# Attention and a bilinear feed-forward on one core: the first eight units' products with v made in pairs, and the early feed-forward columns split around the turning

## The chip, the core and the metric

The kernel runs on one core of one Trainium2 chip. The metric is the device time of one execution in microseconds (us); the kernel before took 1402.33 us (median of three runs, 1402.2 to 1406.92). Five engines work side by side, each through its own list of instructions in order, and wait for one another on semaphores: PE (TensorE, the matrix multiplier), ACT (ScalarE), DVE (VectorE), POOL (GpSimd) and SP, which here only issues DMAs. PE writes to PSUM alone; ACT and DVE fetch its results from there. A difference of 0.5% (about 7 us) is taken as what a measurement of this kernel can tell from no change.

## The reference

For 8 batches of 8 heads, with 576 rows of 64 columns, softmax attention in which a score counts only if it is within tau of its row's maximum; then, with the heads laid side by side (x has 4608 rows and 512 columns), a bilinear feed-forward.

```python
scores = scale * np.matmul(q, k.transpose(0, 1, 3, 2))
thresh = np.max(scores, axis=-1, keepdims=True) - tau
scores = np.where(scores >= thresh, scores, -1000000000.0)
scores = scores - np.max(scores, axis=-1, keepdims=True)
attn = np.exp(scores)
attn = attn / (np.sum(attn, axis=-1, keepdims=True) + 1e-09)
attn_out = np.matmul(attn, v)
...
a = x @ w_a
b = x @ w_b
return (a * b @ w_out)
```

The weights w_a and w_b are 512 by 1536, w_out is 1536 by 512.

## The kernel before

**Units and slots.** Two heads make a pair; there are 32 pairs, four to a batch. A unit is a pair and 128 of its rows (the last 64 rows of two pairs share a unit of their own). The main loop (L1117) goes over units in slots g = 0, 1, 2, ...; the first eight units are pairs 0 to 3 with rows 0 to 127 (g = 0 to 3) and pairs 0 to 3 with rows 128 to 255 (g = 4 to 7). Slot g holds the scores of unit g and later steps of the units before it. Each engine's instructions stand in the order in which the loop issues them (`keep_order`), so the loop fixes the order of every engine's list.

**One slot, for the first units.** In program order:
- `scores` (L389): PE makes the scores of unit g for both heads (L404) in two PSUM tiles; DVE takes the row maxima (L411, one per head) and the threshold (L412).
- for g = 2 to 9, `weighted_unit` (L594) for unit g - 2: `product` (L538) multiplies the turned weights with v in 36 PE matmuls (L546) of 64 moving columns each, a 64 by 64 block of v being the stationary side; ACT fetches the first half of the result (L553, 128x64) and DVE the second in two copies (L554, 64x64), into the feed-forward's input x; POOL copies x with its partition halves exchanged into xS (L569, two copies of 64x128).
- `convert_rest` and `convert_first`: the feed-forward's weights come as 64-bit words of which ACT (L298, L299), POOL (L305, L324) and DVE (L311, L319) make fp32 numbers, two or three pieces a slot in this stretch.
- `weigh` (L422): ACT makes the exponentials (L431, L432), DVE applies the threshold and sums (L435); then DVE's reciprocal.
- `turn_pe` (L472) for unit g - 1 (up to g = 8): PE turns and scales the weights with 18 matmuls against a diagonal matrix (L483) into two PSUM tiles, of which ACT copies the larger (L485) and DVE the smaller (L486). The result is what `weighted_unit` reads in the next slot.
- `diagonals` (L456) on ACT for unit g (L462).
- `advance(pace)` (L1204): feed-forward work on the first block of x, once it is there (from g = 5), by columns: a slot's allowance is 0.04 of a block's columns plus 576, and each product with v takes 576 off. In the first feed-forward steps (L854) PE multiplies the weights with x or xS; ACT fetches the product with w_a (L860), and DVE multiplies in the one with w_b (L862).

From g = 9 on another scheme takes over: the weights are turned by DVE (L502) and DMAs through DRAM, and `advance` stands at four places of a slot.

**PSUM.** All PE results share one pool of four tiles (`banks`, L128), taken in turn. A new tile can be written once the tile taken four before it has been read: so the order in which PE's steps stand decides which copy each step waits for.

**Loads.** SP issues the loads in order: v of a pair (`load_v`, L214) one slot ahead of the pair's first use here, and pieces of weights (`load_weights`, L271) between them, each behind the PE instruction last issued before it.

The functions that the diff touches, and what calls them:

Of the kernel before, what the change touches and what calls it, by code (L numbers as in the profile page):

```python
# [23 lines left out]
BY_PE = 8  # L24
# [30 lines left out]
def kernel(  # L55
# [38 lines left out]
    nc = tc.nc  # L94
    B, H, S, D = q.shape
    P = 128
# [3 lines left out]
    HP = H // 2  # L100
    NT = 4
    MAIN = NT * P
    TAIL = S - MAIN
# [8 lines left out]
    NSLOT = 9  # L112
# [15 lines left out]
    def banks(n, name):  # L128

        return psum.tile([P, 2, 512], FP32, tag="banks", name=name)[:, :, 0:n]  # L130
# [4 lines left out]
    loaded = {}  # L135
# [90 lines left out]
    for f in range(NG):  # L226
        for c in range(HP):
            for dst, w in ((wa_sb, w_a), (wb_sb, w_b)):
                src = []
                for r in range(2):  # L230
                    chunks = [(2 * c + e) % HP * 2 + (r + (c >= HP // 2)) % 2 for e in range(2)]
                    cols = slice(f * CW + r * CH, f * CW + (r + 1) * CH)
                    rows = w[:, cols].bitcast(U32).rearrange("(k p) f -> p k f", p=D)
                    src.append(rows[:, chunks[0]:chunks[1] + 1:2])
                pieces.append((dst[:, f, 2 * c:2 * c + 2].rearrange("p k f -> p (k f)"), src))
    for F in range(NF):
# [3 lines left out]
    state = {"loaded": 0, "added": 0, "converted": 0, "rows": 0, "sums": False, "through": 0, "over": False,  # L240
             "layer": False, "paced": False, "all": False, "turn": 0, "due": NPIECES, "wide": True, "slot": 0, "reading": False, "first": 0}
# [90 lines left out]
    for _ in range(TW_BUFS):  # L332
        t = work.tile([P, 2 * NB, Q], FP32, tag="tw", bufs=TW_BUFS, name="rows")
# [21 lines left out]
    prepared, scored, weights, turned, whole = {}, {}, {}, {}, {}  # L355
    x_of, xtail_of = {}, {}
    ahead, settled, settled_of = {}, {}, {}
    blocks, complete, swaps = [], [], {}
# [113 lines left out]
    def turn_pe(i, u):  # L472

        ws, dg = weights.pop((i, u))
        ws = [w.rearrange("p n e -> p (n e)") for w in ws]
        wT = turned_tile()[:, 0:G].rearrange("p g s e -> p (g s e)").rearrange("p (s w) -> p s w", w=P)
        turned[i, u, "pe"] = [wT[:, :, y * D:(y + 1) * D] for y in range(2)]
        tp = banks(512, "tp").rearrange("p y (s q) -> p y s q", s=NT)
        last = banks(P, "tp")
        for s in range(NSLOT):  # L480
            for j, w in enumerate(ws):
                to = (last[:, 0] if s == 2 * NT else tp[:, s // NT, s % NT])[j * D:(j + 1) * D]
                nc.tensor.matmul(to, w[:, s * D:(s + 1) * D], dg[:, j], start=True, stop=True)  # L483
        for y in range(2):
            nc.scalar.copy(wT[:, y * NT:(y + 1) * NT], tp[:, y])  # L485
        nc.vector.tensor_copy(wT[:, 2 * NT], last[:, 0])  # L486
# [51 lines left out]
    def product(wT, vm, n):  # L538

        pv = banks(n // 2, "pv")  # L540
        for s in range(NSLOT):
            for j in range(2):
                rows = slice(j * D, (j + 1) * D)
                for c in range(2):
                    y = j ^ c
                    nc.tensor.matmul(pv[c * D:(c + 1) * D, y], vm[rows, s], wT[y](rows, s),  # L546
                                     start=(s == 0), stop=(s == NSLOT - 1))
        return pv

    def settle(out, pv, c0, c1, others):  # L550

        n = c1 - c0
        one = [nc.scalar.copy(out[:, 0:n], pv[:, 0, c0:c1])]  # L553
        two = [nc.vector.tensor_copy(out[c * D:(c + 1) * D, n:2 * n], pv[(1 - c) * D:(2 - c) * D, 1, c0:c1])  # L554
               for c in range(2)]
        for mine, theirs in ((one, others[1] + two), (two, others[0] + one)):
            for a in mine:
                for b in theirs:
                    tc.declare_no_dep(a.ins, b.ins, reason="banks of their own")
        others[0].extend(one)  # L560
        others[1].extend(two)

    def x_tile(name):
        return work.tile([P, HP, HALF], FP32, tag="xT", bufs=XT_BUFS, name=name)

    def exchange(x, xs, hp, c0, c1, engine):

        for r in range(2):
            engine.tensor_copy(xs[r * D:(r + 1) * D, hp, c0:c1], x[(1 - r) * D:(2 - r) * D, hp, c0:c1])  # L569
# [21 lines left out]
                    exchange(x_of[key], xs, hp, 0, HALF, nc.gpsimd)  # L591
                ahead[key] = xs, count

    def weighted_unit(i, u):  # L594

        b, hp = pairs[i]
        wT = turned.pop((i, u, "pe"))
        pv = product([lambda rows, s, t=t: t[rows, s] for t in wT], loaded[i]["v"], P)
        settled_of[i] = settled_of.get(i, 0) + P
        if (b, 0) not in x_of:  # L600
            x_of[b, 0] = x_tile("xT")
            state["xs"] = x_tile("xS")
        settle(x_of[b, 0][:, hp, u * P:(u + 1) * P], pv, 0, D, ([], []))
        exchange(x_of[b, 0], state["xs"], hp, u * P, (u + 1) * P, nc.gpsimd)
        if hp == HP - 1:
            state["rows"] = u + 1
            if u == 0:
                blocks.append(((x_of[b, 0], state["xs"]), ("first", b, 0)))

    def tails(x, pv, hp, c0, c1):  # L610

        copies = [(nc.scalar.copy if j == c else nc.vector.tensor_copy)(
            x[j * D:(j + 1) * D, hp + c, c0:c1], pv[c * D:(c + 1) * D, j]) for c in range(2) for j in range(2)]
        for n, a in enumerate(copies):
            for m, b in enumerate(copies[:n]):
                if (n in (0, 3)) != (m in (0, 3)):
                    tc.declare_no_dep(a.ins, b.ins, reason="partitions of their own")

    def weighted_tails(i):

        b, hp = pairs[i]
        flush(("v", i), ("v", i + 1), ("wT", i, 2))
        t = turned.pop((i, NT))
        pv = banks(TAIL, "pv")
        for s in range(NSLOT):
            for j in range(2):
                rows = slice(j * D, (j + 1) * D)
                for c in range(2):
                    nc.tensor.matmul(pv[c * D:(c + 1) * D, j], loaded[i + c]["v"][rows, s],
                                     t[rows, 2 * c:2 * c + 2, s], start=(s == 0), stop=(s == NSLOT - 1))  # L630
        if hp == 0 and b % GT == 0:
            xtail_of[b // GT] = x_tile("xt")
        t = b % GT
        tails(xtail_of[b // GT], pv, hp, t * TAIL, (t + 1) * TAIL)
        for p in (i, i + 1):
            settled_of[p] = settled_of.get(p, 0) + TAIL
            if settled_of[p] == S:
                del loaded[p], prepared[p]
# [385 lines left out]
    def advance(cols):  # L1024
        running["owed"] += cols
        while running["owed"] > 0:
            if running["ffn"] is None:
                exchange_blocks()
                if not blocks:
                    running["owed"] = 0.0  # L1030
                    return
                if len(blocks[0][0]) == 4 and state["first"] == 3 * SEVENS:
                    for group in range(SEVENS):
                        first_sums(3, group)
                    state["first"] += 1
                if state["over"] and not state["all"]:
                    first_sums(3, SEVENS)
                    state["all"] = True
                running["tiles"] = len(blocks[0][0])
                running["ffn"] = ffn(*blocks.pop(0))  # L1040
                running["left"] = cost()
            step, rest, whole = next(running["ffn"], (None, 0, 0))
            if step == 0:
                running["owed"] = 0.0
                return
            if step is None:
                running["ffn"] = None
                state["through"] += 1
            else:
                running["owed"] -= step  # L1050
                running["left"] -= step
                passed(step)
                running["done"] = running["done"] + step if rest else 0
                running["rest"] = rest
                running["room"] = min(ROOM, whole // 2)
# [24 lines left out]
    units = []  # L1080
# [9 lines left out]
    first = {i: g for g, (i, u) in enumerate(units) if u == 0}  # L1090
# [21 lines left out]
    n = 0  # L1112
# [4 lines left out]
    for g in range(len(units) + PV_LAG):  # L1117
# [9 lines left out]
        if BY_PE + 1 < g <= len(units) + 1:  # L1127
            n = g - PV_LAG
# [3 lines left out]
        if here:  # L1132
            i, u = units[g]
# [4 lines left out]
        pace = (PACE if g > BY_PE else PACE_EARLY) * BLOCK_COLS  # L1138
        if g > BY_PE:
            pace = min(pace, backlog() / (min([a for a in arrivals if a > g] + [len(units) + PV_LAG + 1]) - g))  # L1140
        pace += NSLOT * S / (2 * NT + 1) + CATCH_UP * max(backlog() - BLOCK_COLS, 0)
        if 2 <= g < BY_PE + 2:
            weighted_unit(*units[g - 2])
            running["owed"] -= NSLOT * P // 2
        if g < 3:
            prep_copy(*prep_pe(g + 1, "q"))
# [20 lines left out]
        if g < 3:  # L1167
            kT, tp = prep_pe(g + 1, "k")
            nc.scalar.copy(kT.rearrange("p (c k) -> p c k", c=2), tp)
        if 0 < g <= BY_PE:  # L1170
            turn_pe(*units[g - 1])
        if g > BY_PE:
            n = g - PV_LAG
# [27 lines left out]
            normalise(i, u)  # L1201
        convert_rest(g, 1)
        if g <= BY_PE:
            advance(pace)  # L1204
        convert_rest(g, 2)
        for n in early.get(g, [])[1:]:
            convert_first(n)
# [74 lines left out]
```

## Time and profile before

| | us |
|---|---|
| time, median of three runs | 1402.33 |
| time of the profiled execution | 1400.57 |
| its span, first to last instruction | 1398.8 |
| PE busy | 1361.5 (97%) |
| DVE busy | 1013.9 (72%) |
| ACT busy | 680.8 (49%) |
| POOL busy | 492.8 (35%) |

The profiled execution's time is 1.77 us above its span. Busy PE is not PE at its peak, since matmuls are pipelined; a share over the whole span is a mean over stages with different limits. In a timeline line the first number is the start and the second the length in us, xN the number of instructions merged into the line, and the bracket at the end the idle time of the engine just before it with what ended that. PE records a matmul of fp32 numbers twice, so 36 matmuls are 72 records.

### The profile page before, as it was taken

Reading aid. Unit: us, or ns where it says so; the run is one execution under the profiler, and the core shown is the slowest. Engines: PE = TensorE matmul, PEld = TensorE weight load, DVE = VectorE, ACT = ScalarE, POOL = GpSimd, SP = SyncE. Lnnn points to the kernel's source line nnn. Section 1 sums busy time; section 2 is a strip of 40 time slices with the busy share of each in tenths; the row PEclk is TensorE's granted clock in tenths of the full one; section 3 lists DMA queues with packets and bytes.
Section 4 is the critical chain, followed back from the end, with each engine's and each line's share of the span. In section 5 each row is a group of like instructions: output and inputs, shape, how many; then the busy total and the mean of one; then the engine's idle time right before and its main releaser. Section 6 shows DMA issues by size and latency. Waiting matters only on the chain.

```text
span 1398.8 us, 76307 instructions
## 1 busy us (share of the span) xinstructions
PE 1361.5 (97%) x33836; PEld 1258.5 (90%) x33836; DVE 1013.9 (72%) x2205; ACT 680.8 (49%) x1248; POOL 492.8 (35%) x675
## 2 busy tenths in 40 slices
PE   7889999999999999999999999999999999999998
PEld 5677588999998799999999999998899998799998
DVE  6999877787777768786767776778777776745425
ACT  6977555545554555544454545454545455431110
POOL 2764543424150607060515142332515060708100
PEclk9999999999999999999999999999999999999999
DMA  9977876667666775676556775566656775550000
GB/s 211 241 212 223 204 206 173 174 170 187 174 154 168 190 192 155 176 190 160 143 143 160 186 180 159 136 190 169 181 130 161 199 190 154 137 146 19 4 19 18
DMA packets 327449, 223.21 MB, mean 160 GB/s; under 512 B 171600, under 2 KB 311632, under 8 KB 327120
## 3 DMA queue, kind: packets, MB, share of 16 engines
q1 hardware_dynamic: 323936, 216.95, 60.1%
q8 instruction: 266, 4.36, 1.3%
q10 hardware_dynamic: 3184, 1.38, 0.4%
q14 instruction: 63, 0.52, 0.1%
HBM read 128.58 MB, written 89.65 MB: 156 GB/s over the span
## 4 chain that ended last, share of the span: by engine, by line
PE 88%; DMA 5%; DVE 4%; SPq 2%; issue 1%; ACT 1%; ACTq 0%; DVEq 0%
PE pab L750 29%; PE po L920 22%; PE pab L854 18%; PE sc L404 9%; PE pv L546 9%; SPq L144 1%; DMA vm<-in_v_dram 1%; DMA wT<-swap 1%; DVE tw L435 1%; DVE mx L411 1%; DMA more_u<-in_moe_w_a_dram 1%; DVE low L311 0%; DMA more_u<-in_moe_w_b_dram 0%; DVE tw L502 0%; DMA sums_u<-in_k_dram 0%
## 5 line engine op out<-in xcount | busy, mean ns | idle before, releaser
L454 ACT ACTIVATE tw<-tw,rcp 128x576 f32<-128x576 f32 x272 | 196.1, 768 | 201.3 <-DVE rcp L448 201.3
L411 DVE TENSOR_REDUCE mx<-sc 128x1 f32<-128x576 f32 x288 | 204.6, 752 | 121.2 <-PE sc L404 120.9
L432 ACT ACTIVATE tw<-sc,bias,scalars 128x576 f32<-128x576 f32 x288 | 239.6, 832 | 10.4 <-DMA qT<-in_q_dram 0.4
L712 POOL TENSOR_TENSOR h<-h,u 128x512 f32<-128x512 f32 x28 | 35.2, 1277 | 590.4 <-DVE h L824 414.1
L435 DVE SCALAR_TENSOR_TENSOR tw<-sc,thr,tw 128x576 f32<-128x576 f32 x288 | 220.9, 797 | 12.3 <-ACT tw L432 11.9
L920 PE MATMUL po<-wo_sb,h 64*64 64x256 f32 (+1 forms) x3408 | 210.5, 367 | 0.0
L502 DVE STREAM_TRANSPOSE tw<-tw 128x576 f32<-128x576 f32 x272 | 194.4, 752 | 0.8 <-ACT tw L454 0.8
L920 PEld LDWEIGHTS po<-wo_sb,h 64*64 64x64 f32 x3408 | 169.8, 133 | 14.9
L404 PE MATMUL sc<-kT,qT 64*64 64x288 f32 x2016 | 170.3, 404 | 1.8 <-issue 0.9
L546 PE MATMUL pv<-wT,vm 64*64 64x128 f32 (+2 forms) x4896 | 164.0, 275 | 3.7 <-DMA vm<-in_v_dram 1.4
L546 PEld LDWEIGHTS pv<-wT,vm 64*64 64x64 f32 x4896 | 153.2, 133 | 12.0 <-issue 4.0
L920 PE MATMUL po<-sums_u,h 64*64 64x256 f32 x2448 | 156.6, 376 | 0.0
L883 POOL TENSOR_TENSOR h<-h 128x256 f32<-128x256 f32 x168 | 117.2, 731 | 110.9 <-PE po L920 106.1
L750 PE MATMUL pab<-xU,wb_sb 64*64 64x128 f32 x4352 | 137.8, 269 | 0.0
L920 PEld LDWEIGHTS po<-sums_u,h 64*64 64x64 f32 x2448 | 126.1, 133 | 12.3 <-DVE h L862 0.5
L750 PEld LDWEIGHTS pab<-xU,wb_sb 64*64 64x64 f32 x4352 | 133.3, 133 | 1.8 <-ACT h L806 0.5
L404 PEld LDWEIGHTS sc<-kT,qT 64*64 64x64 f32 x2016 | 108.8, 133 | 17.3 <-issue 4.9
L431 ACT ACTIVATE bias<-mx,scalars 128x1 f32<-128x1 f32 x288 | 82.7, 287 | 66.1 <-DVE mx L411 65.6
L553 ACT COPY xT<-pv 128x128 f32<-128x128 f32 (+1 forms) x68 | 17.6, 259 | 193.5 <-PE pv L546 193.5
L750 PE MATMUL pab<-xS,wa_sb 64*64 64x128 f32 x2176 | 108.5, 269 | 0.8 <-issue 0.8
L554 DVE COPY xT<-pv 64x128 f32<-64x128 f32 (+1 forms) x136 | 38.1, 280 | 80.5 <-PE pv L546 79.0
L535 ACT COPY kept<-po 128x512 f32<-128x512 f32 x65 | 34.8, 535 | 120.3 <-PE po L920 106.4
(163 smaller groups left out, 2468.7 us busy)
## 6 DMA issues: line engine op xcount, KB each, us to landing
wT<-swap SPq DMA_DIRECT2D x242, 288.0 KB, 3.8
swap<-tw SPq DMA_DIRECT2D x480, 144.0 KB, 3.1
vm<-in_v_dram SPq DMA_DIRECT2D x128, 72.0 KB, 2.6
swap<-tw SPq DMA_DIRECT2D x128, 72.0 KB, 2.9
kT<-in_k_dram SPq DMA_DIRECT2D x112, 72.0 KB, 3.2
wT<-swap SPq DMA_DIRECT2D x56, 144.0 KB, 3.6
out_dram<-kept SPq DMA_DIRECT2D x27, 256.0 KB, 3.7
qT<-in_q_dram SPq DMA_DIRECT2D x112, 40.0 KB, 2.8
```

The lines of the kernel that those rows point to most:

```text
L404: nc.tensor.matmul(sc[m][o * D:o * D + wide, c], qT[r, q0:q0 + wide], kT[r, c * SH:(c + 1) * SH], start=True, stop=True)
L411: nc.vector.tensor_reduce(mx[:, c], sc[j], axis=AX.XY, op=ALU.max)
L431: nc.scalar.activation(bias[:, j:j + 1], mx[:, j:j + 1], AF.Copy, scale=e_nscale)
L432: nc.scalar.activation(wb[j], sb[j], AF.Exp, bias=bias[:, j:j + 1], scale=e_scale)
L435: nc.vector.scalar_tensor_tensor(out=wv, in0=sb[j], scalar=thr[:, j:j + 1], in1=wv, op0=ALU.is_ge, op1=ALU.mult, accum_out=sums[:, j:j + 1])
L454: nc.scalar.activation(w, w, AF.Copy, scale=rcp[:, j:j + 1])
L502: nc.vector.transpose(w, w)
L546: nc.tensor.matmul(pv[c * D:(c + 1) * D, y], vm[rows, s], wT[y](rows, s), start=(s == 0), stop=(s == NSLOT - 1))
L750: nc.tensor.matmul(out[c * D:(c + 1) * D, r, f * P:(f + 1) * P], w[g][k][rows, w0:w0 + D], moving[k][rows], start=(fresh and k == 0 and f ...
L854: nc.tensor.matmul(pab[c:c + columns(), r], w[rows, f // n, k, fs + c:fs + c + columns()], moving, start=(k == 0), stop=(k == H - 1))
L883: (nc.vector if state["over"] else nc.gpsimd).tensor_tensor(*a, **kw)
L920: nc.tensor.matmul(po[c * D:(c + 1) * D, r, y, cut], ht[rows, t0:t0 + D], other[rows, f, cut], start=(f == 0), stop=(f == NF // 2 - 1))
```

## The change

**Products in pairs.** Units (i, u) and (i + 1, u) of two neighbouring pairs are now multiplied with v together, in slots 3, 5, 7 and 9, and slots 2, 4, 6 and 8 have no product. `by_pairs` makes 36 matmuls of 128 columns for both units: output partitions 0 to 63 belong to the first pair and 64 to 127 to the second, where before they were two halves of one unit's columns. The result is fetched as `tails` (L610) does it: two copies of 64x128 by ACT and two by DVE for a pair of units. POOL exchanges both pairs at once, in two copies of 64 x 2 x 128. The feed-forward's allowance is still lessened by 576 in every slot from 2 to 9. `weighted_tails` calls `by_pairs` too, with what it did before.

**Feed-forward columns.** Up to slot 8, `advance(pace)` behind the turning becomes `advance(pace / 2)` ahead of `turn_pe` and `advance(pace / 2)` at the old place.

```diff
@@ turn_pe
-        turned[i, u, "pe"] = [wT[:, :, y * D:(y + 1) * D] for y in range(2)]
+        turned[i, u, "pe"] = wT
@@
-    def weighted_unit(i, u):
+    def weighted_units(i, u):
         b, hp = pairs[i]
-        wT = turned.pop((i, u, "pe"))
-        pv = product([lambda rows, s, t=t: t[rows, s] for t in wT], loaded[i]["v"], P)
-        settled_of[i] = settled_of.get(i, 0) + P
+        wT = [turned.pop((i + c, u, "pe")) for c in range(2)]
+        pv = by_pairs(P, i, lambda rows, c, s: wT[c][rows, s])
...
-        settle(x_of[b, 0][:, hp, u * P:(u + 1) * P], pv, 0, D, ([], []))
-        exchange(x_of[b, 0], state["xs"], hp, u * P, (u + 1) * P, nc.gpsimd)
-        if hp == HP - 1:
+        x, xs, cols = x_of[b, 0], state["xs"], slice(u * P, (u + 1) * P)
+        tails(x, pv, hp, cols.start, cols.stop)
+        for r in range(2):
+            nc.gpsimd.tensor_copy(xs[r * D:(r + 1) * D, hp:hp + 2, cols], x[(1 - r) * D:(2 - r) * D, hp:hp + 2, cols])
+        for p in (i, i + 1):
+            settled_of[p] = settled_of.get(p, 0) + P
+        if hp + 1 == HP - 1:
...
+    def by_pairs(n, i, moving):
+        pv = banks(n, "pv")
+        for s in range(NSLOT):
+            for j in range(2):
+                rows = slice(j * D, (j + 1) * D)
+                for c in range(2):
+                    nc.tensor.matmul(pv[c * D:(c + 1) * D, j], loaded[i + c]["v"][rows, s], moving(rows, c, s),
+                                     start=(s == 0), stop=(s == NSLOT - 1))
+        return pv
@@ main loop
         if 2 <= g < BY_PE + 2:
-            weighted_unit(*units[g - 2])
+            if g % 2:
+                weighted_units(*units[g - 3])
             running["owed"] -= NSLOT * P // 2
...
+        if g <= BY_PE:
+            advance(pace / 2)
         if 0 < g <= BY_PE:
             turn_pe(*units[g - 1])
...
         if g <= BY_PE:
-            advance(pace)
+            advance(pace / 2)
```

From slot 10 on, the lists of all engines are the same as before, with the same waits.

More of the change, by code (lines that the diff above doesn't have):

```diff
@@ L602, in weighted_unit @@
             state["xs"] = x_tile("xS")
-        settle(x_of[b, 0][:, hp, u * P:(u + 1) * P], pv, 0, D, ([], []))
-        exchange(x_of[b, 0], state["xs"], hp, u * P, (u + 1) * P, nc.gpsimd)
-        if hp == HP - 1:
+        x, xs, cols = x_of[b, 0], state["xs"], slice(u * P, (u + 1) * P)
[5 more added lines that the diff above has]
+        if hp + 1 == HP - 1:
             state["rows"] = u + 1
             if u == 0:
-                blocks.append(((x_of[b, 0], state["xs"]), ("first", b, 0)))
+                blocks.append(((x, xs), ("first", b, 0)))
+    def by_pairs(n, i, moving):
[7 more added lines that the diff above has]
+        return pv
     def tails(x, pv, hp, c0, c1):
@@ L623, in weighted_tails @@
         t = turned.pop((i, NT))
[L624 to L630, printed above, removed]
+        pv = by_pairs(TAIL, i, lambda rows, c, s: t[rows, 2 * c:2 * c + 2, s])
         if hp == 0 and b % GT == 0:
```

## Prediction

> **What bounds the kernel now.** I read the busy tenths by slices first, for where time is lost.
>
> ```profile
> PE   7889999999999999999999999999999999999998
> ...
> DVE  6999877787777768786767776778777776745425
> ...
> PE 88%; DMA 5%; DVE 4%; SPq 2%; issue 1%; ACT 1%; ACTq 0%; DVEq 0%
> ```
>
> PE is full from the fourth slice of 35 us on, and the chain of waits is PE for 88%. PE idles 37 us in all (1398.8 - 1361.5). Then the busy time by stages of 20 us, to see who holds the beginning (columns: busy us of PE, PEld (weight loads), DVE, ACT, POOL with counts; PE clock; DMA share; GB/s).
>
> ```profile
> 40.00:60.00 20.00, 15.00 (x349) 13.07 (x341) 19.19 (x41) 17.42 (x37) 15.33 (x20) 1.00 1.09 237
> 60.00:80.00 20.00, 16.48 (x339) 14.63 (x337) 19.57 (x45) 17.86 (x37) 15.46 (x18) 0.96 0.84 231
> 80.00:100.00 20.00, 17.94 (x316) 16.05 (x314) 18.42 (x38) 15.00 (x31) 13.51 (x14) 0.96 0.71 205
> 100.00:120.00 20.00, 18.57 (x284) 17.03 (x282) 19.40 (x40) 15.69 (x31) 10.84 (x11) 1.00 0.87 252
> ```
>
> Up to about 140 us DVE is the bound: 19.19 and 19.57 of 20 us busy, where PE has 15.00 and 16.48. Slots 2 to 9, the ones changed, lie between 22 and 91 us. So a change there is worth what it takes from DVE's list or from DVE's few waits; PE time saved there lies beside DVE. From slot 10 on all lists and waits are as before, so whatever is won or lost by slot 9 shifts the rest as a whole: DVE stays busy up to 141 us, and then PE runs a fixed amount of work to the end.
>
> The timeline shows the two waits of DVE that matter, one in slot 3 and one in slot 9.
>
> ```profile
> 32.87 1.26 PE L546 MATMUL pv<-wT,vm 64*64 64x64 f32 x68 [0.56 <-DMA vm<-in_v_dram]
> ...
> 34.18 0.46 DVE L554 COPY xT<-pv 64x64 f32<-64x64 f32 x2 [0.66 <-PE pv L546]
> ```
>
> ```profile
> 78.36 2.08 PE L854 MATMUL pab<-xT,wa_sb 64*128 64x128 f32 x16 [1.45 <-DVE tw L435]
> ...
> 80.20 1.81 PE L854 MATMUL pab<-xS,wa_sb 64*128 64x128 f32 x16
> ...
> 83.89 1.42 DVE L411 TENSOR_REDUCE mx<-sc 128x1 f32<-128x576 f32 x2 [1.43 <-PE sc L404]
> ```
>
> In slot 3 the product waits for v of pair 1, and DVE for the product. In slot 9 DVE waits 1.43 us for scores, because PE before them ran at half clock: these groups of 16 records take 1.16 and 1.06 us elsewhere. The granted clock says so:
>
> ```profile
> 77.00:78.00 1.00, 0.00 (x0) 0.00 (x0) 1.00 (x3) 1.00 (x3) 0.86 (x3) 1.00 0.75 307
> 78.00:79.00 1.00, 0.64 (x6) 0.67 (x8) 1.00 (x5) 0.89 (x3) 1.00 (x2) 0.66 0.01 4
> 79.00:80.00 1.00, 1.00 (x13) 1.00 (x13) 0.93 (x3) 0.77 (x2) 0.57 (x1) 0.50 0.00 0
> ```
>
> The clock (third figure from the end) falls to 0.50 after PE had stood still for 0.96 and 1.45 us with 0.44 us of work between.
>
> **The change part by part.**
>
> *PE.* Eight products of 64 columns take 1.28 us each, 10.2 us; four of 128 columns take 2.20 us each (the row of 72 such records at 113.27 us), 8.8 us. The saving of 1.4 us lies where DVE is the bound: nothing by itself.
>
> *DVE's copies.* Each product of a unit cost two copies of 64x64, 0.46 us, 0.49 with the gap behind. A pair of units costs two of 64x128, 0.59 us (the row at 139.14 us), 0.62 with the gap. So slots 2, 4, 6, 8 lose 0.49 us of DVE and slots 3, 5, 7, 9 gain 0.13.
>
> *ACT's copies.* Two of 64x128 instead of one of 128x64 (208 ns) in the odd slots, none in the even ones. No row has 64x128 by ACT; 64x64 takes 0.21 and 128x128 0.27 us, so two take 0.42 to 0.54. ACT gains 0.2 to 0.3 us in an odd slot and loses 0.2 in an even one: in sum 0, I take 0.
>
> *POOL's copies.* Sixteen of 64x128 (509 ns mean) become eight with 256 elements per partition; rows of 64x256 have 401 ns. Bounds 0.40 to 1.02 us each, 3 to 8 us for 8.1. POOL is not the bound. DVE's L311 and L319 beside POOL's copies take 0.69 and 0.52 us, where 0.60 and 0.42 is usual, so each even slot may give back 0.2 us: 0 to -0.8 in sum; I take -0.5.
>
> *The products' wait, slot 3.* Of the changed product's 36 matmuls 33 need pair 1's second half of v or come behind one that does. It landed at 32.87, from a DMA issued in slot 0, ahead of all that is changed. So the product ends at 32.87 + 33/36 x 2.20, near 35.0, not 34.13, and DVE's copies start 0.87 later. The 0.49 us that slot 2 saved is lost in this wait. In slot 5 v of pair 3 (issued at 36.03, median landing 7.7 us) is there by 44, ahead of the product at 46: hidden, with 2 us to spare.
>
> *DVE's ledger* against the trace (plus is later). Slot 3: +0.87 + 0.13 = +1.0. Slot 4: -0.49, +0.5. Slot 5: +0.13; but there DVE waited 0.11 and 0.22 us for exponentials, and ACT for a DMA until 47.55, which does not move: +0.4 (between +0.3 and +0.6). Slot 6: -0.49; but DVE's multiply L862 (0.33 us) moves ahead of the conversions; at its old place it stood in time that the second L319 (1.49 us instead of 0.42) spent on POOL's L324 anyway. So +0.33: +0.25. Slot 7: +0.4. Slot 8: -0.1. DVE comes to slot 9 as in the trace.
>
> *The split allowance.* It gives the same columns per slot (24, 16, 16 and 24 matmuls in slots 5 to 8), with 8 of them ahead of the turning. PSUM tiles are taken in another order: the last matmuls of the turning now wait for DVE's first L435 in slots 5 to 8. In slot 8 the first eight fill the time behind the scores, but the turning ends near 74.5 and its last matmuls wait for L435 at 78.2: PE stands still for some 3.7 us, longer than before. Behind them come two groups of 16 records where three had been. At half clock (1.84 and 1.63 us from start to start) scores of slot 9 run from 82.1 to 83.3, the 128-column product to 85.5; DVE's copies wait for it and end at 86.05, against 86.07 in the trace. DVE's 1.43 us move from the scores to the product: gain 0. At full clock (1.0 and 0.9) the scores run from 80.5, the product ends at 83.9, DVE is the later with 84.1, and its copies end at 84.7: gain 1.35.
>
> Here the Trainium skill speaks against the change: "TensorE: Matmul & The Clock Gate", the section "Why this matters for your kernels", wants no idle gaps of PE over about 3 us between bursts, as one idle window brings back the half clock. The rows agree that idle time comes first (0.96 and 1.45 us sufficed). By the rule the longer gap keeps the clock low and the sum is the first of the two; without it the second.
>
> *Moved past queues.* The weight loads on SP are tied to PE's latest instruction; in even slots it is the scores, not the product (1.3 us earlier), in slots 5 to 8 the turning's later end (up to 2 us later). ACT waited for a weight DMA only once (0.72 us at 47.55), so I take 0, between -0.7 and +1.
>
> **Sum.** -0.1 at slot 9, 0 for the slot itself, -0.5 beside POOL: -0.6 us. From the profiled execution's 1400.57 that gives 1400.0; its median is 1.76 higher, so 1402.33 - 0.6 = **1401.7**.
>
> **Rivals.**
> 1. *The clock stays full in slot 8*: another 1.35 us, 1400.4. For it: the clock held in other gaps of PE (2.25 us at 58.44). Against: 3.7 us is the longest gap.
> 2. *POOL's lighter work frees DVE*: five L319 of 1.49 to 1.51 us fall to 0.42, 5.4 us, 1401.7 - 5.4 = 1396.3. Against: each of them runs against the L324 that DVE's own L319 of the piece before releases, so they keep meeting. The Trainium skill ("SBUF — State Buffer", section "Who interferes with whom") makes this an exclusive lock of DVE's second port pair; the rows' lengths agree.
> 3. *Slower: ACT becomes the bound.* The first eight matmuls stand ahead of the turning and take 1.16 us; in slot 5 they also wait for the copies of the product, so ACT gets L485 about 1.1 us later. If ACT passes on 1.16 us in each of four slots, 4.6 us; DVE feels it once ACT's lag passes 1.65 us (exponential ready at 57.72, used at 59.37): 4.6 - 1.65 = +3.0, 1404.7 with the forecast's -0.6. For it: ACT is busy 17.4 and 17.9 of 20 us. Against: slot 6 has no product to wait in and turns 2 us earlier, giving the lag back (ACT idled 1.67 us there).
>
> **Chances.** Forecast 0.55, rival 1 0.17, rival 2 0.09, rival 3 0.19. Range 1397.5 to 1405.5: it holds all but rival 2, with the open costs of the loads (1 us) and of POOL. By 0.5%, about what a measurement of this kernel can tell from no change, faster would be below 1395.3, slower above 1409.3; no case reaches either. I leave 0.05 and 0.04 for what I have not seen, 0.91 for within 0.5%.
>
> **What would show it.** Right: DVE still over 95% busy from 40 to 80 us; its copies in slot 3 waiting about 2 us; the clock low near 78 us; DVE waiting in slot 9 for the product; the tail merely shifted. Wrong: ACT idle gone and DVE waiting for exponentials (rival 3); L319 at 0.42 in slots 6 to 9 (rival 2); any stage behind 145 us changed by itself, which would break the claim that only the beginning counts.

## The result

The changed kernel took 1408.55 us (median of nine runs, 1406.86 to 1411.19), the kernel before 1402.33 on the same chip (nine runs, 1400.98 to 1407.58): ratio 1.0038, 95% interval 1.0023 to 1.0053. That is slower by less than 0.5%, but outside the predicted range and to the other side. The profiled execution took 1411.19 us with a span of 1409.4; it is 10.6 us behind the profiled one of before, more than the 6.2 us between the medians, so single steps read from the two traces overstate the change.

The page of the changed kernel, busy tenths and the chain of waits:

```profile
PE   7889999999999999999999999999999999999998
...
DVE  5999877787777777776767776777767776745424
...
PE 89%; DVE 4%; DMA 2%; SPq 2%; ACT 2%; issue 1%; POOL 0%; DVEq 0%; ACTq 0%
```

By this page nothing has moved: PE is full from the same slice on, and the shares of the chain differ little (DMA 2%, where it was 5%). The stages of 20 us that bounded the beginning (columns as in the prediction; the clock is the third figure from the end):

```profile
40.00:60.00 20.00, 17.52 (x256) 15.62 (x256) 19.06 (x39) 19.02 (x41) 14.68 (x16) 0.91 1.09 242
60.00:80.00 20.00, 15.52 (x240) 13.87 (x240) 18.78 (x37) 15.98 (x34) 14.28 (x15) 0.91 0.87 223
80.00:100.00 20.00, 18.64 (x308) 16.95 (x308) 18.15 (x37) 16.48 (x33) 14.58 (x15) 0.91 0.66 163
100.00:120.00 20.00, 17.68 (x276) 15.94 (x274) 19.43 (x44) 14.18 (x29) 9.84 (x11) 1.00 0.94 263
```

DVE lost 0.1 to 0.8 us in each of the first three stages, and the clock is 0.91 in three stages where it was 0.96 to 1.00. The timeline shows where, in slots 2 and 3 and in slots 8 and 9:

```profile
26.92 1.14 PE L378 MATMUL tp<-more_u,sums_u 96*128 96x96 f32 x6 [1.75 <-ACT bias L431]
28.00 3.34 PE L483 MATMUL tp<-first_u,tw 128*64 128x128 f32 x36
31.39 0.29 DVE L486 COPY wT<-tp 128x128 f32<-128x128 f32 x1 [1.42 <-PE tp L483]
32.45 2.37 PE L620 MATMUL pv<-wT,vm 64*64 64x128 f32 x72
34.85 0.61 DVE L626 COPY xT<-pv 64x128 f32<-64x128 f32 x2
...
80.27 0.44 PE L483 MATMUL tp<-first_u,tw 128*64 128x128 f32 x4 [3.64 <-DVE tw L435]
...
81.66 1.93 PE L862 MATMUL pab<-xT,wb_sb 64*128 64x128 f32 x16
83.36 2.04 PE L404 MATMUL sc<-kT,first_u 64*128 64x288 f32 x8
85.36 1.42 DVE L411 TENSOR_REDUCE mx<-sc 128x1 f32<-128x576 f32 x2 [0.97 <-PE sc L404]
87.60 0.61 DVE L626 COPY xT<-pv 64x128 f32<-64x128 f32 x2 [0.56 <-PE pv L620]
```

In three of the four even slots, which have no product now, PE stands still (1.75 us in slot 2, 2.71 in slot 6, 3.64 in slot 8), and matmuls behind that run at half clock: the turning of slot 2 takes 3.34 us, the scores of slot 9 2.04 (1.24 at full clock), and DVE waits for both.

To see where the rest went, I set the start of one and the same instruction of each slot (DVE's threshold, L412) in the two traces against each other. The changed kernel is 0.35 us late in slot 0, ahead of all changes, and 2.04 us late in each of the slots 10 to 17, in which nothing moves. Then slot 21 begins another 2.98 us late, and some ten steps of 0.3 to 1.0 us follow along the way (and one of -0.9), to 9.24 us in slot 143. All of that lies in code that the change leaves alone. The step ahead of slot 21, in the kernel before and in the changed one (SP's lines are its DMA issues, xN so many in a row; PE's line waits for the second `wT<-swap`):

```profile
159.48 1.83 SPq L144 DMA_DIRECT2D swap<-tw  x4
161.40 1.19 SPq L144 DMA_DIRECT2D wT<-swap  x2
162.64 3.35 SPq L144 DMA_DIRECT2D kT<-in_k_dram  x4
166.09 1.21 SPq L144 DMA_DIRECT2D wT<-swap  x2
...
170.42 2.08 PE L546 MATMUL pv<-wT,vm 64*64 64x128 f32 x67 [1.09 <-DMA wT<-swap]
```

```profile
160.70 3.21 SPq L144 DMA_DIRECT2D swap<-tw  x4
164.01 0.93 SPq L144 DMA_DIRECT2D wT<-swap  x2
164.98 2.59 SPq L144 DMA_DIRECT2D kT<-in_k_dram  x4
167.67 1.08 SPq L144 DMA_DIRECT2D wT<-swap  x2
...
173.56 3.75 PE L546 MATMUL pv<-wT,vm 64*64 64x128 f32 x67 [2.40 <-DMA wT<-swap]
```

The same four issues of `swap<-tw` take 3.21 us instead of 1.83. PE waits 2.40 instead of 1.09 us for the transfer, and the product takes 3.75 instead of 2.08. The stages of 1 us of the changed kernel say what the DMA engines and the clock do (last three columns: clock, DMA share, GB/s):

```profile
163.00:164.00 1.00, 1.00 (x13) 0.61 (x9) 0.97 (x3) 0.85 (x2) 0.00 (x0) 1.00 0.19 40
...
174.00:175.00 1.00, 1.00 (x28) 1.00 (x24) 0.59 (x1) 0.00 (x0) 0.00 (x0) 0.50 0.50 88
```

Behind the late issue the DMA engines run nearly empty (0.19), and behind PE's wait the clock is at half. The longer wait (1.31 us) and the slower product (1.67 us) make up the 2.98 us of slot 21. One of the four issues holds SP for 1.83 us alone; the timeline of that stretch, and its DMA packets by queue (packets, MB, share):

```profile
161.61 1.83 SPq L144 DMA_DIRECT2D swap<-tw  x1
```

```profile
q8 instruction: 1, 0.02, 4.5%
```

Beside the issue stands one packet of the queue that the page calls instruction.

The pages count such packets for the whole span; before, then after:

```profile
q8 instruction: 266, 4.36, 1.3%
```

```profile
q8 instruction: 264, 4.33, 1.3%
```

They are 16.4 KB each (4.36 MB / 266). PE's list, matmuls, weight loads and waits together, has 68,241 instructions in the trace of before, which makes 256.5 to a packet; after, 67,670 for 264, 256.3. So I take q8 to carry PE's code, a piece of 256 instructions at a time. The change takes 144 matmuls out of the list, each two matmul records and two weight loads, 571 instructions with the waits. All that comes behind is the same, but its pieces begin 571 instructions, two pieces and 59 instructions, further on in the program. A shift by whole pieces leaves the boundaries where they were, so only the rest counts. I call the number of instructions by which a kernel's list is longer than that of before, up or down to the range 0 to 255 by whole pieces, its **place**: before 0, after 197 (three pieces, 768, less 571).

### The profile page after: what moved, and what is told of

It reads as the page before. It is cut to its first block, busy times and chain, and to the rows that moved or that the text cites. A ratio compares the mean times of both kernels' runs of the same rounds, so it can differ in the third digit from the quotient of the medians.

```text
span 1409.4 us, 75715 instructions
## 1 busy us (share of the span) xinstructions
PE 1369.8 (97%) x33548; PEld 1254.8 (89%) x33548; DVE 1011.5 (72%) x2197; ACT 681.4 (48%) x1248; POOL 491.2 (35%) x667
## 3 DMA queue, kind: packets, MB, share of 16 engines
q10 hardware_dynamic: 3184, 1.38, 0.4%
## 4 chain that ended last, share of the span: by engine, by line
PE 89%; DVE 4%; DMA 2%; SPq 2%; ACT 2%; issue 1%; POOL 0%; DVEq 0%; ACTq 0%
PE pab L758 30%; PE po L928 22%; PE pab L862 18%; PE sc L404 9%; PE pv L546 9%; SPq L144 1%; DVE tw L435 1%; DMA wT<-swap 1%; PE tp L483 1%; DVE mx L411 0%; DVE tw L502 0%; DVE low L311 0%; ACT tw L432 0%; DMA raw<-in_moe_w_a_dram 0%; DVE wb_sb L319 0%
## 5 line engine op out<-in xcount | busy, mean ns | idle before, releaser
L928 PE MATMUL po<-wo_sb,h 64*64 64x256 f32 (+1 forms) x3408 | 214.1, 367 | 0.0
L928 PEld LDWEIGHTS po<-wo_sb,h 64*64 64x64 f32 x3408 | 172.8, 133 | 14.5
L404 PE MATMUL sc<-kT,qT 64*64 64x288 f32 x2016 | 174.7, 404 | 3.1 <-issue 1.7
L546 PE MATMUL pv<-wT,vm 64*64 64x128 f32 (+1 forms) x4320 | 156.5, 284 | 3.5 <-DMA wT<-swap 2.4
L546 PEld LDWEIGHTS pv<-wT,vm 64*64 64x64 f32 x4320 | 146.8, 134 | 8.2 <-issue 3.3
L758 PE MATMUL pab<-xS,wa_sb 64*64 64x128 f32 x2176 | 112.3, 269 | 0.7 <-issue 0.7
L553 ACT COPY xT<-pv 128x128 f32<-128x128 f32 x60 | 15.9, 265 | 196.3 <-PE pv L546 196.3
L758 PE MATMUL pab<-xT,wa_sb 64*64 64x128 f32 x1856 | 95.6, 269 | 0.0
L554 DVE COPY xT<-pv 64x128 f32<-64x128 f32 x120 | 34.6, 288 | 84.3 <-PE pv L546 83.0
```

What stands on the lines that cost most here:

```text
L404: nc.tensor.matmul(sc[m][o * D:o * D + wide, c], qT[r, q0:q0 + wide], kT[r, c * SH:(c + 1) * SH], start=True, stop=True)
L758: nc.tensor.matmul(out[c * D:(c + 1) * D, r, f * P:(f + 1) * P], w[g][k][rows, w0:w0 + D], moving[k][rows], start=(fresh and k == 0 and f ...
L928: nc.tensor.matmul(po[c * D:(c + 1) * D, r, y, cut], ht[rows, t0:t0 + D], other[rows, f, cut], start=(f == 0), stop=(f == NF // 2 - 1))
```

## Experiments

All were timed in five rounds (12 runs each, but 6 of e10 and 10 of e18) beside the kernel before on the same chip; times differ between chips (1402 there, 1408 to 1411 on these), so ratios are given. "Slot 10" and "slot 21" are read from one trace each against the first trace of before: how late slot 10 is, and by how much slot 21 adds to that of slot 20. "Issue" is the longest of the four `swap<-tw` issues ahead of slot 21. The table is sorted by place, which is worked out from the trace's count of PE's instructions. "15 twice" means that 15 matmuls of the first turnings are made twice; the diff stands below.

| run | kernel | place | ratio, 95% interval | slot 10 | slot 21 | issue |
|---|---|---|---|---|---|---|
| e1 | before, unchanged | 0 | 0.9989, 0.997 to 1.0007 | +2.0 | +0.4 | 0.44 |
| e5 | after, 15 twice | 1 | 1.0004, 0.9986 to 1.0021 | +3.9 | +0.2 | 0.50 |
| e11 | after, 79 twice | 1 | 1.0014, 0.9992 to 1.0036 | +1.8 | +0.9 | 0.49 |
| e15 | pairs only, 15 twice | 2 | 1.0002, 0.9983 to 1.0022 | +4.5 | +0.4 | 0.44 |
| e16 | before, 8 twice | 31 | 0.9994, 0.9973 to 1.0014 | +1.1 | +0.4 | 0.44 |
| e17 | after, 23 twice | 33 | 1.0007, 0.9992 to 1.0022 | +1.3 | +0.2 | 0.44 |
| e12 | before, 16 twice | 63 | 1.0036, 1.0016 to 1.0056 | -0.4 | +0.9 | 1.93 |
| e8 | before, 32 twice | 126 | 1.0042, 1.0019 to 1.0065 | +3.5 | -0.1 | 1.80 |
| e6 | after, 47 twice | 129 | 1.0036, 1.0017 to 1.0056 | -0.3 | +0.1 | 0.47 |
| e7 | before, 49 twice | 191 | 1.0048, 1.0022 to 1.0074 | +1.2 | +3.4 | 1.44 |
| e2 | after, unchanged | 197 | 1.0042, 1.002 to 1.0064 | +2.6 | +4.0 | 1.93 |
| e10 | after, 64 twice | 197 | 1.0048, 1.0034 to 1.0062 | +0.9 | +1.5 | 1.38 |
| e13 | after, 15 more at slot 24 | 197, then 1 | 1.0036, 1.0017 to 1.0054 | +2.4 | +2.8 | 1.49 |
| e14 | after, 15 more at slot 84 | 197, then 1 | 1.0048, 1.0029 to 1.0068 | +3.8 | +0.9 | 1.05 |
| e3 | pairs only | 198 | 1.0043, 1.002 to 1.0066 | +2.5 | +1.6 | 1.68 |
| e18 | before, 56 twice | 218 | 1.0031, 1.0011 to 1.005 | +4.5 | -0.8 | 0.45 |
| e4 | split only | 250 | 1.0015, 0.9995 to 1.0035 | +0.9 | +0.7 | 0.48 |
| e9 | before, 64 twice | 250 | 1.0018, 1.0003 to 1.0033 | +2.9 | +0.1 | 0.45 |

**Copies, and one part alone.** e1 and e2 are the two kernels unchanged. e3 takes out the split (diff against the changed kernel), e4 is the kernel before with the split alone:

```
-        if g <= BY_PE:
-            advance(pace / 2)
         if 0 < g <= BY_PE:
             turn_pe(*units[g - 1])
...
-            advance(pace / 2)
+            advance(pace)
```

> The kernel before, unchanged, for the spread of its times and a second trace. Theory L (the late loss is a two-way event: PE's product at 172 us waits for a DMA and the clock then falls to 0.50, which the kernel before meets in some executions and the changed one in nearly all): times in two groups near 1402 and 1407, the upper one at a lower mean clock, and about a third of the runs in the upper. Theory S (the late loss comes from the change itself and is the same in every execution; the kernel before never has it): one group near 1402 in trace and clock, the values near 1407 spread without a clock that goes with them.

> The changed kernel, unchanged, for a second trace. Both theories: 1407 to 1411. Theory L: the shift at slot 10 stays near +2 us in each trace, and the jump of +3 us at slot 21 is there in a trace near 1408 to 1411 and missing or smaller in one of 1407 or less. Theory S: the jump is there in every trace with the same size within 0.5 us.

> Only the pairing; the whole allowance stays behind the turning. If the wait of the turning's last matmuls for DVE (2.71 us in slot 6, 3.64 us in slot 8 of the changed kernel) comes from the split, these waits are short or gone here, the clock stays up at 61 and 82 us, slots 7 and 9 lose nothing, and the shift at slot 10 is +0.5 us instead of +2: 1403 to 1405. If the half clock comes from the even slots that have no product, the dips at 61 and 82 us and +2 us stay: 1407 to 1410.

> Only the split; products unit by unit as before. If the split makes the loss: the shift at slot 10 is +1 to +2 us, and the time 1404 to 1409. If the pairing makes it: the shift is within 0.5 us of the kernel before and the time 1401 to 1404. Without the pairing every slot has a product, so PE stands still for a shorter time in front of the turning's last matmuls.

Theory L fell: there are no two groups (copies of before between 1405.29 and 1412.05 without a gap), and the upper times have no lower clock. Theory S held in so far as the step at slot 21 was there again; but it was +4.0 us and not within 0.5 us of 2.98, as the theory wanted. The early loss of 2.04 us turned out to be within what traces of one kernel differ by: the unchanged kernel before was 2.01 us late in slot 10 in its second trace. e3 has the whole loss, e4 little of it, so it goes with the pairing. But it does not go with the half clock, the reason that I gave: the dips of the clock in slots 6 and 8 (60 to 64 and 80 to 84 us) are there in e3, but the kernel before has such dips too in its second trace (e1, half clock from 57.8 to 61.3 and from 78.3 to 85.1 us); and the shift of e3 at slot 10, +2.5 us, is hardly more than two traces of one kernel differ by. What e3 has in common with the changed kernel is PE's list, shorter by 570 instructions; e4's has 6 fewer. The q8 packet beside the long issue then gave theory P: the place decides.

**The place, moved by itself.** To move it, I make some of the turning's matmuls twice, in both kernels; the second gives the same values, and PE has time there. The number by unit is the only difference between these kernels (here e5):

```
+        for n in range(([2, 2, 2, 2, 2, 2, 2, 1])[units.index((i, u))]):
+            s, j = n // 2, n % 2
+            nc.tensor.matmul(tp[j * D:(j + 1) * D, s // NT, s % NT], ws[j][:, s * D:(s + 1) * D], dg[:, j], start=True, stop=True)
         for s in range(NSLOT):
```

> The changed kernel with 15 matmuls of the first turnings made twice (2 in each of the first seven, 1 in the eighth; the second one gives the same values). The change takes 571 instructions from PE's list, which is loaded in pieces of 16 KB, 256 instructions; 15 matmuls are 60 instructions, so that the pieces begin at the same instructions behind slot 9 as before the change (511 fewer, two pieces less one instruction). Theory P (the loads of PE's code meet other DMAs than before, and that makes the late loss of about 4 us): the jump at slot 21 is below 1 us, and the time is that of the kernel before plus the early loss of up to 2 us, ratio 1.000 to 1.002. Theory E (the late loss follows from the early one, wherever the pieces begin): ratio 1.004 as for the changed kernel.

> As the run with 15, but with 47 matmuls made twice (6 in each of the first seven turnings, 5 in the eighth): the pieces of code begin half a piece away from those of the kernel before. Theory P: a time of its own, the same as for the kernel before moved by half a piece, plus the early loss of up to 2 us. Theory E: ratio 1.004; the added matmuls cost nothing, as PE has time in the first slots.

> The kernel before with 49 matmuls of the first turnings made twice (7 in each of seven): 196 more instructions of PE, so that its pieces of code begin where those of the changed kernel begin behind slot 9 (there 571 fewer, which is 197 more up to whole pieces). Theory P: the jump at slot 21 comes back (1.5 us or more) with an issue on SP of 1.7 to 1.9 us among the transfers that the product in slot 21 waits for, and the ratio is 1.002 to 1.004. Theory E: the kernel before with nothing lost, ratio 0.999 to 1.001.

> The kernel before with 32 matmuls made twice (4 in each of the eight turnings): half a piece of code later. Theory P: a time that differs from the kernel before's by anything up to 5 us, and the run with 47 above it by the early loss of up to 2 us. Theory E: ratio 0.999 to 1.001.

Theory E, by which the late loss follows from the early one, fell with e5 and e7. With its place put back, the changed kernel has lost nothing (1.0004), although its trace is 3.9 us late in slot 10. With the changed kernel's place the kernel before loses as much as the change (1.0048, where I expected 1.002 to 1.004), although nothing else of the change is in it. Its trace shows the same long issue, again with a q8 packet in it, and the same late product; in e5 the four issues take 1.88 us and PE waits 1.27. First e7, then e5:

```profile
160.31 2.81 SPq L144 DMA_DIRECT2D swap<-tw  x4
163.22 0.96 SPq L144 DMA_DIRECT2D wT<-swap  x2
164.22 2.59 SPq L144 DMA_DIRECT2D kT<-in_k_dram  x4
166.92 1.34 SPq L144 DMA_DIRECT2D wT<-swap  x2
...
173.11 2.87 PE L549 MATMUL pv<-wT,vm 64*64 64x128 f32 x67 [2.78 <-DMA wT<-swap]
```

```profile
163.81 1.88 SPq L144 DMA_DIRECT2D swap<-tw  x4
165.79 1.10 SPq L144 DMA_DIRECT2D wT<-swap  x2
166.94 3.25 SPq L144 DMA_DIRECT2D kT<-in_k_dram  x4
...
175.01 2.08 PE L549 MATMUL pv<-wT,vm 64*64 64x128 f32 x67 [1.27 <-DMA wT<-swap]
```

The size of the step hangs on the clock as well. In the traces of the changed kernel, e2, e7 and e13 PE waited 2.21 to 3.37 us in slot 21, the clock fell to 0.50 behind that, and the step is 2.8 to 4.0 us; in e3 and e10 PE waited as long (2.70 and 2.54 us), the clock stayed at 1.00, and the step is 1.6 and 1.5 us.

e6 and e8, half a piece away from before, agree with each other (1.0036 and 1.0042) as theory P wants it of two kernels with one place, and are slower too. But e7 and e8 left a rival, W: that the added matmuls cost the time.

**Whole pieces.** The next four add whole pieces, or a quarter:

> The kernel before with 64 matmuls of the first turnings made twice (8 in each): 256 instructions of PE, one whole piece of code, so that the pieces begin at the same instructions as before. Theory P (where PE's pieces of code begin decides): ratio 0.998 to 1.001, although this is the most work added. Theory W (the added matmuls themselves cost time, which is why 32 and 49 of them were slower by 0.4 to 0.5%): ratio 1.005 or more.

> The changed kernel with 64 matmuls made twice: the pieces of code stay where the change put them, and PE stands still less in the first slots, so that its clock stays up there. Theory P: the early loss goes (slot 10 within 0.7 us of the kernel before), the late one stays with its jump at slot 21; ratio 1.002 to 1.004. If the half clock of the first slots were the cause of all: ratio 0.999 to 1.001.

> The changed kernel with 79 matmuls made twice (10 in each of seven turnings, 9 in the eighth): one whole piece more than the run with 15, so that the pieces begin as in the kernel before, and the clock stays up in the first slots. Theory P: neither loss; slot 10 within 0.7 us of the kernel before or ahead of it, no jump at slot 21, ratio 0.998 to 1.001. Theory W: 1.005 or more.

> The kernel before with 16 matmuls made twice (2 in each): a quarter of a piece of code later, the one quarter not yet seen (0: ratio 1.000; a half: 1.004; three quarters: 1.004 to 1.005). Theory P gives no figure, only a time that may differ from the kernel before's by up to 0.5% to either side. Theory W: 1.001, a quarter of what 64 cost.

W fell: 64 matmuls, the most that the kernel before was given, cost 1.0018 (its place is 250 and not 0, as six waits of PE fell away) and 16 cost 1.0036. By the same comparison of 64 and 0, added matmuls may cost some 0.1 to 0.2%, more than I expected of e9 (0.998 to 1.001) and e11; but e4, at the same place and without added matmuls, has 1.0015, so that the place may account for it. I also expected slot 10 of e10 and e11 within 0.7 us of the kernel before; it was 0.9 and 1.8 us late, inside the spread of two traces. A piece more in the changed kernel leaves its loss as it was (e10, 1.0048); a piece and the place put back, and it is gone (e11, 1.0014).

e6 and e10 also fill the stillness of PE in slot 8 and so test the half clock. Stages and timeline of e6:

```profile
82.00:83.00 1.00, 1.00 (x20) 0.61 (x20) 1.00 (x1) 1.00 (x3) 0.98 (x1) 1.00 0.40 86
83.00:84.00 1.00, 1.00 (x48) 1.00 (x44) 1.00 (x3) 1.00 (x3) 0.65 (x1) 1.00 0.87 254
```

```profile
79.18 0.44 PE L486 MATMUL tp<-first_u,tw 128*64 128x128 f32 x4 [2.50 <-DVE tw L435]
...
81.44 1.24 PE L404 MATMUL sc<-kT,first_u 64*128 64x288 f32 x8
82.61 2.19 PE L623 MATMUL pv<-wT,vm 64*64 64x128 f32 x72
...
83.19 1.41 DVE L411 TENSOR_REDUCE mx<-sc 128x1 f32<-128x576 f32 x2
```

After a gap of 2.50 us instead of 3.64 the clock stays at 1.00, the scores take 1.24 us, DVE waits for nothing, and the slot is 1.83 us shorter than in the trace of before. The total is slower all the same (1.0036): the half clock of the beginning is real and does not decide the time.

**Where it arises, and how wide the good place is.** e13 and e14 put 15 small matmuls ahead of the scores of slot 24 or 84, whose results the scores overwrite:

```
+            for n in range(15 if units.index((i, u)) == 24 and (c, t, j) == each[0] else 0):
+                nc.tensor.matmul(sc[m][o * D:o * D + wide, c, 0:D], qT[r, q0:q0 + wide], kT[r, 0:D], start=True, stop=True)
```

> The changed kernel with 15 small matmuls (64 moving columns, their results overwritten by the scores) ahead of the scores of slot 24: the pieces of PE's code begin as in the kernel before only behind slot 24, and the added matmuls cost about 1 us of PE. If the 5 us that hang on the pieces arise by slot 24 (the jump at slot 21 is 3 to 4 us of them): ratio 1.004 to 1.005, no gain. If they arise behind it, all along the way: 1.001 to 1.002.

> The same at slot 84, past the middle of the time. If the loss arises by slot 24: ratio 1.004 to 1.005. If it arises all along the way: 1.003, between the changed kernel and the run with 15 at the beginning.

> Only the pairing, with 15 matmuls of the first turnings made twice, so that the pieces of code begin as in the kernel before. Theory P: ratio 1.000 to 1.0015, as for both parts of the change with 15. If the pairing has a cost of its own beside the pieces: 1.003 or more.

> The kernel before with 8 matmuls of the first turnings made twice (1 in each): 32 instructions, an eighth of a piece later. No theory gives a figure: between the place of the kernel before (1.000) and a quarter of a piece later (1.0036). It shows how narrow the good place is.

> The changed kernel with 23 matmuls of the first turnings made twice: 92 instructions, so that PE's pieces of code begin 33 instructions behind the place of the kernel before, where that kernel with 8 matmuls more had a ratio of 0.9994. Theory P: 0.999 to 1.001; if this is lower than with 15, it is the best version of the change. Without theory P: 1.004.

> The kernel before with 56 matmuls made twice (7 in each): 224 instructions, between the place of the changed kernel (197, ratio 1.004) and the kernel before (256, ratio 1.000). Theory P: any ratio between 1.000 and 1.005; it shows on which side the good place ends. Theory W (the added matmuls cost time): 1.005.

Put back at slot 24 the place gains little (1.0036), at slot 84 nothing (1.0048). With 0.0007 (my 1 us) for the added matmuls, e13 would be 1.0011 (e5's 1.0004 and 0.0007) if all of the loss arose behind slot 24. Its own interval leaves that out, but e5's is as wide, and the two together just allow it: that a good part arises by slot 24 is likely and not shown. The pairing by itself costs nothing at the good place (1.0002), and the changed kernel at 33 is as good as at 1 (1.0007). No version was measurably faster than the kernel before. The eight kernels with places from 250 over 0 to 33 lie between 0.9989 and 1.0018, those from 63 to 198 between 1.0036 and 1.0048, and 218 is between (1.0031).

**What stays open.** Only the step at slot 21 is followed from the packet to the wait, and only for places 191 to 198; it is not the whole loss there either (e14 has 1.0048 with a step of 0.9 us). Where the other places lose their 0.3 to 0.4% I have not found: e6, e8 and e18 have no step at slot 21, and e8 and e12 have the long issue and only -0.1 and +0.9 us there. Why a packet of code holds an issue up is not shown either, only that they stand together, and that through all 20 traces: of 2353 `swap<-tw` issues with such a packet in the same time, 1049 took over 1 us, of the 9807 others 28. Each trace has 46 to 62 of these long issues at whatever place, so what the place can change is which issues they are, and not how many. The kernels at good places have such a packet here too, on an issue that the table leaves out. In the trace of before the packet fell on the first `kT` issue, which took 1.19 us where the others took 0.63 to 0.77; in e11, e15, e16 and e17 it fell on the first `wT<-swap` (2.09, 1.64, 1.54 and 1.19 us, about 0.4 without it), and slot 21 lost 0.2 to 0.9 us.

## Why the prediction was wrong

**The step that failed** stands after the table of stages: "From slot 10 on all lists and waits are as before, so whatever is won or lost by slot 9 shifts the rest as a whole". The lists are as before; where the pieces in which PE's list is loaded begin is not (place 197), and that alone is worth the loss: 1.0042 with it, 1.0004 with the place put back, 1.0048 in the kernel before with that place. The range left that out altogether: each of its cases was a sum over slots 2 to 9. The page had the figure that was needed, 266 packets of instruction on q8, and the counts of PE's matmuls and weight loads (33,836 each) beside it. The prediction had named what would show the error, "any stage behind 145 us changed by itself", and slot 21 did.

With the place put back, the forecast of a ratio of 0.9996 (0.6 us less) stands beside 1.0004 (0.9986 to 1.0021) and 1.0007 (0.9992 to 1.0022): that the change's own work comes to about nothing was right. By its steps:

- *Products.* Four of 72 records (2.37 us in slot 3, 2.19 in slot 9; 2.20 forecast), hidden as said.
- *DVE's copies.* 289 ns each, as in the row they were taken from: right.
- *ACT's copies.* 260 ns each, 2.1 us in all for 1.7: +0.4 where I took 0.
- *POOL's copies.* 695 ns each, 5.6 us in all for 8.1, inside the bounds of 3 to 8. But DVE's L319 on wa_sb and wb_sb between 22 and 100 us took 16.6 us (15.9 before): +0.8 where I took -0.5. The locked ones stayed at 1.49 to 1.51 us, so rival 2 was wrong.
- *Slot 3.* Product's end at 34.82 (35.0 forecast), but not for the reason given: it began at 32.45, as slot 2 was late, and v of pair 1 had landed by 32.60, so that no wait for it shows. DVE's copies did not wait 2 us there either, as the prediction's signs had it.
- *Slot 2.* Left out of the ledger. Without the product PE waited 1.75 us for ACT there, and the turning ran at half clock; DVE waited 1.42 us.
- *Slots 8 and 9.* A gap of 3.64 us (3.7 forecast) and half clock behind it. DVE then waited 0.97 us for the scores and 0.56 for the product; the forecast had 1.43 for the product alone. The rule of the Trainium skill ("TensorE: Matmul & The Clock Gate", section "Why this matters for your kernels") fits these gaps: 3.64 us brought half clock, the 2.50 us of e6 did not. It does not fit all: 1.75 us in slot 2 and 2.40 us in slot 21 brought half clock too, and 2.70 us in slot 21 of e3 did not.
- *Rival 1* is e6 and e10: the clock stayed up, slot 8 was 1.83 and 1.82 us shorter than before, and slots 8 and 9 together took 1.2 us less than in the changed kernel (1.35 forecast).
- *Rival 3.* DVE waited 0.4 to 0.6 us for exponentials in slots 3, 5 and 7: ACT did not become the bound.

The early sum was -0.1 us at slot 9 against +2.04 in slot 10 of the trace. As the unchanged kernel's own traces differ by 2.0 there, this neither proves nor refutes the ledger, and it did not decide the time.

## What to carry to other kernels

A kernel like this one, whose busiest engine has a list of 68,241 instructions, can change its time by 0.4% because an early edit moved the pieces in which that list is loaded. Before an early edit is given the credit or the blame for a few us, count by how many instructions the list of the busiest engine has changed, make up the rest to a whole piece with idle work, and measure again; and take a second trace of the unchanged kernel before reading a single late slot.

## What the runs showed of the hardware

- PE's code comes in packets of 16.4 KB, 256 instructions, on a queue of its own (q8), mostly every 3 to 12 us. That it is PE's own follows from the counts alone: 256.5 and 256.3 of PE's instructions to a packet. The Trainium skill ("Runtime: NRT & Kernel Launch", section "Instruction fetch mechanics") has the size and holds the cost of a boundary to be mostly hidden. The size agrees; here the place of the boundaries is worth 0.3 to 0.5% of the time.
- A DMA issue on SP that had such a packet beside it took 1.05 to 1.93 us in eight of the runs above, where its neighbours took 0.36 to 0.50. Over all 20 traces 45% of the `swap<-tw` issues with a packet in the same time took over 1 us, and 0.3% of the others.
- In the changed kernel's trace the granted clock changes only at multiples of 3.41 us from 23.58 us on (27.00, 30.41, 40.65, ..., 173.77), and single gaps do not tell when. Up to 200 us it fell five times: four times behind a step of 3.41 us in which PE was busy for 0.71 to 1.66 us, and once (40.65) behind one with 2.69 us; it stayed up behind one with 1.85 us.
- One kernel's times spread more than I took for granted: the kernel before took 1402.25 to 1419.11 us in 35 runs on one chip, and its median was 1402.33 on one chip and 1408.67 to 1410.80 on others.
